# Late q tiles through DRAM, and re-timed loads and transposes around two attention turns

## The chip, the cores and the metric

The kernel runs on one core of a Trainium2 chip. The metric is the device time of one execution in microseconds (us), median of several runs. Five engines work side by side, each in the order of its own program: TensorE (PE, with weight loads shown as PEld), VectorE (DVE), ScalarE (ACT), GpSimd (POOL) and SyncE (SP). SP's queue (SPq) issues nearly all transfers (DMA), also those that transpose on the way. ACT's queue issues some.

## The reference, cut to what matters

One layer on 2048 tokens of width 640, forward and backward: linear attention with 32 heads of 20, then a gated MLP of width 1728, each behind a layer norm and with a residual. The outputs are the layer's result and the gradients for x, wqkv, wo, w1, w3 and w2.

```python
q, k, v = split_heads(layernorm(x) @ wqkv)
phi = lambda t: jnp.where(t > 0, t + 1, jnp.exp(t)) + 1e-6
pq, pk = phi(q), phi(k)
kv  = einsum("bhsd,bhse->bhde", pk, v)          # one 20x20 block per head
z   = einsum("bhsd->bhd", pk)
num = einsum("bhqd,bhde->bhqe", pq, kv)
den = einsum("bhqd,bhd->bhq", pq, z)[..., None] + 1e-6
h   = x + (num / den).reshape(S, D) @ wo
n   = layernorm(h)
out = h + (silu(n @ w1) * (n @ w3)) @ w2
# and the vjp of out for grad_out, in A_x, wqkv, wo, w1, w3, w2
```

The kernel never forms num. It makes r = pq / den for each tile of 128 tokens, and one matrix W' = blockdiag(kv) @ wo, so that the attention's result is r @ W'. In the backward pass Q' = r^T @ g_h takes the place of the sums over q: the gradient of kv, that of wo and the matrix for k's gradient come out of it.

## The kernel before

All is one program; the order of the Python calls is the order in each engine's queue. Tiles of a tag share buffers; `bufs` says how many. A new tile of a tag waits until the last reader of the buffer's previous tile is done. The forward turn begins when the last k tile is done: M = pk^T @ xn is formed in five blocks, transposed to mT by DMA, and kv follows from it.

```python
pqs[t] = p1.tile([P, D], BF16, name="pq", bufs=5)            # q tiles 0 to 4
...
def r_prod(t):                                              # POOL: pq * z
    for j in range(2):
        pr[t, j] = pf.tile([P, HD], F32, name="pr", tag="h2", bufs=3)
        G.tensor_tensor(out=pr[t, j][:], in0=pqs[t][:, js], in1=Zb[:, js], op=ALU.mult)

def r_rest(t):                                              # DVE: den, 1/den, r
    for j in range(2):
        V.reduce_sum(out=den[:, j * 16:(j + 1) * 16], in_=heads(pr.pop((t, j))[:]), axis=AX.X)
    V.tensor_scalar(out=den[:], in0=den[:], scalar1=1e-6, scalar2=None, op0=ALU.add)
    V.reciprocal(out=rden[:, t, :], in_=den[:])
    V.tensor_tensor(out=heads(pqs[t][:]), in0=heads(pqs[t][:]),
                    in1=rden[:, t, :].unsqueeze(2).to_broadcast([P, H, DH]), op=ALU.mult)

def r_out(t):                                               # SP: r^T for the product, r for later
    dmaT(out=pqT[:, :, t * P:(t + 1) * P], in_=pqs[t][:])
    dma(out=r_v[:, t, :], in_=pqs.pop(t)[:])

def q_late(t):                                              # q tiles 5 to 15
    pqs[t] = pf.tile([P, D], BF16, name="pql", bufs=4)
    for j in range(2):
        p1_half(acc[:, 0:HD], t, j * HD)                    # PE, 5 matmuls of 128x320
        A.activation(mq[:, js], acc[:, 0:HD], AF.Exp)
        A.activation(rq[:, js], acc[:, 0:HD], AF.Relu)
    V.tensor_scalar(out=mq[:], in0=mq[:], scalar1=1.0, scalar2=1e-6, op0=ALU.min, op1=ALU.add)
    V.tensor_tensor(out=pqs[t][:], in0=mq[:], in1=rq[:], op=ALU.add)

def f2_Wp():                                                # W' transposed, all five at the end
    for i in range(DT):
        dmaT(out=Wp[:, :, i * P:(i + 1) * P], in_=wTs[0][:, i, :])
    ...
# f2_at(t): x += r @ W' (PE, ACT or DVE), then statistics (DVE, POOL)
# f2_hn(t): layer norm (DVE), stored; f2_ht(t): its transposition (PE for t < 4, else DMA)
run((q_late, 5), (q_late, 6), (r_rest, 4), (q_late, 7), (r_out, 4), (r_prod, 5), (f2_kv, 3), (f2_kv, 4), (q_late, 8),
    (r_rest, 5))
Wp = U1.tile([P, DT, D], BF16, name="Wp", tag="W6")         # wo's buffer
run((f2_wT, 0), ..., (f2_wT, 4), (f2_Wp,), (r_out, 5), (r_prod, 6), (q_late, 9),
    (r_rest, 6), (r_out, 6), (r_prod, 7), (q_late, 10), (r_rest, 7), (r_out, 7), (r_prod, 8), (q_late, 11),
    (mlp_ghh, 4), (r_rest, 8), (f2_at0, 0), ..., (f2_hn, 0), (r_out, 9), ..., (f2_ht, 0), ...)
```

The MLP follows in four chunks of 512 tokens, 14 steps (`fc`) each. In chunk 0, `r_prod`, `r_rest` and `r_out` of tiles 12 to 15 stand between the steps; chunk c computes the attention of chunk c + 1.

In the backward pass, after the MLP's gradients, 16 tiles give g_h and g_q. Then Q' is summed (`q_parts`), and its transposition QT, wo, kvN (kv's) and W's parts are loaded or transposed for what follows:

```python
dmaT(out=woT, in_=A_wo[:, :])
load_xnT(0); load_wqT(2); load_xnT(1)
dmaT(out=kvN[:], in_=kvT_d[:, :])
... part(...)                                               # q_parts: each finished m issues dmaT(QT[m])
next(jobs)                                                  # a weight-gradient job: 16 matmuls of 128x320
for i in range(DT):
    dwoT.append(br.tile([P, D], BF16, name="dwoT", bufs=2))
    unload(square(qp, kvN, i), dwoT[i][:], (A.copy, V.tensor_copy)[i % 2])
    dmaT(out=dwo[:, :, i * P:(i + 1) * P], in_=dwoT[i][:])
A.dma_start(out=out3S, in_=dwo[:])
next(jobs)
for m, (a, b) in enumerate(M_H):                            # gkvT = wo^T-block @ QT
    acc = d_acc()[:, 0]                                     # tag dkv, three buffers, as in square()
    ...; masked(gkvT, acc[:, 0:n], m)
...
for i in range(DT):
    unload(square(wqT[:, 2 * DT:, :], gkvT, i), gm[:, i, :], ...)
    dmaT(out=wqT[:, 2 * DT:, i * P:(i + 1) * P], in_=gm[:, i, :])
for m in range(DT):
    dmaT(out=gkv_b[:, :, m * P:(m + 1) * P], in_=gkvT[:, m, :])
for t in range(ST):                                         # the g_k loop: xn @ gm, jobs between;
    ...                                                     # at t = 2, 5, 8, 11, 14: square(mN, gkv_b, n)
```

Of the kernel before, what the change touches and what calls it, by code (L numbers as in the profile page):

```python
# [50 lines left out]
SQ = _pieces(M_H, SPLIT_D, DH)  # L51


@with_exitstack
def kernel(
# [22 lines left out]
    def rows(ap):  # L78
        return ap.rearrange("(t p) d -> p t d", p=P)
# [9 lines left out]
    dram = ctx.enter_context(tc.tile_pool(name="dram", bufs=1, space=bass.MemoryType.DRAM))  # L89
    r_d = dram.tile([S, D], BF16, name="r_d")  # L90
# [4 lines left out]
    kvT_d = dram.tile([D, D], BF16, name="kvT_d")  # L95
    hn_d = dram.tile([S, D], BF16, name="hn_d")
    hh_d = dram.tile([F, S], BF16, name="hh_d")
    gg_d = dram.tile([2 * F, S], BF16, name="gg_d")
    r_v, pk_v, xn_v, hn_v, m_v = rows(r_d), rows(pk_d), rows(xn_d), rows(hn_d), rows(m_d)
# [117 lines left out]
    mT = p1.tile([P, DT, D], BF16, name="mT")  # L217
# [82 lines left out]
    def r_prod(t):  # L300

        for j in range(2):
            js = slice(j * HD, (j + 1) * HD)
            pr[t, j] = pf.tile([P, HD], F32, name="pr", tag="h2", bufs=3)
            G.tensor_tensor(out=pr[t, j][:], in0=pqs[t][:, js], in1=Zb[:, js], op=ALU.mult)
# [35 lines left out]
    mbs = pf.tile([P, 4, D], BF16, name="mbs", tag="hnT")  # L341
# [9 lines left out]
    def m_end(m):  # L351
        mb = mbs[:, m % 4, :]
        acc = macc.pop(m)
        for j in range(2):
            A.copy(out=mb[:, j * HD:(j + 1) * HD], in_=acc[j][:, 0:HD])
        dmaT(out=mT[:, :, m * P:(m + 1) * P], in_=mb)
        dma(out=m_v[:, m, :], in_=mb)
# [101 lines left out]
    m_part(2, range(8))  # L459
    z_sum(*zz)  # L460
    r_prod(0)
    m_part(2, range(8, ST))
    m_end(2)
    r_rest(0)
    r_prod(1)
    p1_kv(0)
    m_part(3, range(8))
    r_out(0)
    r_rest(1)
    r_prod(2)  # L470
    m_part(3, range(8, ST))
    m_end(3)
    p1_kv(1)
    r_out(1)
    r_rest(2)
    r_prod(3)
    m_part(4, range(8))
    p1_kv(2)
# [32 lines left out]
    def q_late(t):  # L511

        mq, rq = (p1.tile([P, D], BF16, name=n, bufs=b) for n, b in (("mq", 3), ("rq", 4)))
        pqs[t] = pf.tile([P, D], BF16, name="pql", bufs=4)
        for j in range(2):
            acc = ps.tile([P, 512], F32, name="mm", bufs=4)
            js = slice(j * HD, (j + 1) * HD)
            p1_half(acc[:, 0:HD], t, j * HD)
# [4 lines that stand above are left out]
# [3 lines left out]
    def f2_wT(i):  # L526

        if i == 0:
            wTs[0] = p1.tile([P, DT, D], BF16, name="wTs", tag="pk")
        acc = [ps.tile([P, 512], F32, name="wt", tag=("o2", "at")[i % 2], bufs=2) for _ in range(2)]  # L530
        for c, a, b, bank, off, first in SQ:
            T.matmul(acc[bank][:, off:off + (b - a) * DH], lhsT=wo[:, c, i * P:(i + 1) * P],
                     rhs=bd[:, c, a * DH:b * DH], start=first, stop=True, skip_group_check=True)
        for bank, (a, b), eng in ((0, (0, SPLIT_D), A.copy), (1, (SPLIT_D, H), V.tensor_copy)):
            eng(out=wTs[0][:, i, a * DH:b * DH], in_=acc[bank][:, 0:(b - a) * DH])

    def f2_Wp():
        for i in range(DT):
            dmaT(out=Wp[:, :, i * P:(i + 1) * P], in_=wTs[0][:, i, :])
        dma(out=rows(wT_d), in_=wTs[0][:])  # L540
        dma(out=rows(kvT_d), in_=bd[:])

# [5 lines left out]
    def f2_ht(t):  # L548
        c, i = divmod(t, TPC)
        if i == 0:  # L550

            hnT[c] = (pf.tile([P, DT, W], BF16, name="hnT", tag="hnT") if c == SC - 1 else pqT[:, :, c * W:(c + 1) * W])
        if t >= TPC:
            dmaT(out=hnT[c][:, :, i * P:(i + 1) * P], in_=hn[t][:])
            return
        tr = ps.tile([P, DT, P], BF16, name="trh", tag="mm", bufs=4)
        for d in range(DT):
            T.transpose(tr[:, d, :], hn[t][:, d * P:(d + 1) * P], ident[:])
        A.copy(out=hnT[c][:, :, i * P:(i + 1) * P], in_=tr[:])
# [76 lines left out]
    def o2_steps(c, q=dma, tag="o2"):  # L636
# [4 lines left out]
        for n, (i, j, fc) in enumerate(jobs):  # L641
            if fc == 0:
                o2["ps"] = ps.tile([P, 512], F32, name="o2", tag=tag, bufs=2)
                if j == 0:
                    o2["sb"] = pf.tile([P, D], BF16, name="h2", bufs=3)
# [25 lines left out]
    def run(*steps):  # L671
# [3 lines left out]
    run((q_late, 5), (q_late, 6), (r_rest, 4), (q_late, 7), (r_out, 4), (r_prod, 5), (f2_kv, 3), (f2_kv, 4), (q_late, 8),  # L675
        (r_rest, 5))
    Wp = U1.tile([P, DT, D], BF16, name="Wp", tag="W6")
    run((f2_wT, 0), (f2_wT, 1), (f2_wT, 2), (f2_wT, 3), (f2_wT, 4), (f2_Wp,), (r_out, 5), (r_prod, 6), (q_late, 9),
        (r_rest, 6), (r_out, 6), (r_prod, 7), (q_late, 10), (r_rest, 7), (r_out, 7), (r_prod, 8), (q_late, 11),
        (mlp_ghh, 4), (r_rest, 8), (f2_at0, 0), (r_out, 8), (r_prod, 9), (q_late, 12), (f2_at0, 1), (r_rest, 9), (f2_hn, 0),  # L680
        (r_out, 9), (r_prod, 10), (q_late, 13), (f2_ht, 0), (f2_at0, 2), (f2_x, 4), (r_rest, 10), (f2_hn, 1),
        (r_out, 10), (r_prod, 11), (q_late, 14), (f2_ht, 1), (f2_at0, 3), (f2_hn, 2), (w2T_rest, 8 * P), (mlp_ghh, 5),
        (r_rest, 11), (r_out, 11), (q_late, 15), (f2_ht, 2), (f2_hn, 3), (f2_x, 6), (mlp_ghh, 6), (load_g2T, 1), (f2_ht, 3),
        (mlp_ghh, 7))
# [20 lines left out]
    for c in range(SC):  # L705
# [8 lines left out]
        for fc in range(FT):  # L714
# [13 lines left out]
            if c == 0 and fc >= 2 and fc < 14:  # L728
                u, k = divmod(fc - 2, 3)
                (r_prod, r_rest, r_out)[k](12 + u)  # L730
# [11 lines left out]
            if c == SC - 1 and fc == 9:  # L742
                wT2 = U1.tile([P, DT, D], BF16, name="wT2", tag="W6")
                dma(out=wT2[:], in_=rows(wT_d))
# [100 lines left out]
    gkv_b = bd  # L845
# [25 lines left out]
    def ln_bwd(acc, t, nrm, st, out, res, pl):  # L871

        gs = pl.tile([P, D], BF16, name="gs", bufs=2)
# [11 lines left out]
        def rest():  # L885
            y = pl.tile([P, D], BF16, name="y")
            A.activation(out=y[:], in_=wb[:], func=AF.Identity, bias=s[:, 3:4], scale=st.rs[:, t:t + 1])  # L887
            V.tensor_tensor(out=out, in0=y[:], in1=res, op=ALU.add)
# [83 lines left out]

    b_load(0)
    b_load(1)
    for t in range(ST):
        g = b_ghn(t)

        def part():
            next(g, None)
# [21 lines left out]
        if t >= 4:  # L1001
            load_xn(t - 4, t - 3)


    tri = U1.tile([P, 3 * DT, D], BF16, name="tri", tag="S0")
    woT, QT, qp = (tri[:, k * DT:(k + 1) * DT, :] for k in range(3))
    kvN = br.tile([P, DT, D], BF16, name="kvN")
# [7 lines left out]
    part()  # L1015
    ln_rest.pop(a)()
# [6 lines left out]
    dmaT(out=woT, in_=A_wo[:, :])  # L1023
    load_xnT(0)
    load_wqT(2)
    load_xnT(1)
    dmaT(out=kvN[:], in_=kvT_d[:, :])
    b_gT(b)
# [8 lines left out]
    part(3)  # L1037
    load_xnT(2)
    load_xnT(3)
# [5 lines left out]
    obs = U1.tile([P, OB], BF16, name="obs", tag="W6")  # L1045
# [28 lines left out]
    jobs = wq_jobs((0,))  # L1074

# [16 lines left out]
    dwo = br.tile([P, DT, D], BF16, name="dwo")  # L1092
    dwoT = []
    for i in range(DT):
        dwoT.append(br.tile([P, D], BF16, name="dwoT", bufs=2))
        unload(square(qp, kvN, i), dwoT[i][:], (A.copy, V.tensor_copy)[i % 2])
        dmaT(out=dwo[:, :, i * P:(i + 1) * P], in_=dwoT[i][:])
    A.dma_start(out=out3S, in_=dwo[:])
    next(jobs)
# [12 lines left out]
    mN, gkvT, gm = (small[:, n:n + DT] for n in (0, DT, 2 * DT))  # L1112
    gzd = small[:, 3 * DT, :].rearrange("p (m q) -> p m q", q=P)
    G.memset(gkvT, 0.0)
    gzb = dx.tile([P, D], F32, name="gzb")
    for m, (a, b) in enumerate(M_H):
        n = (b - a) * DH
        acc = d_acc()[:, 0]
        for c in range(DT):
            T.matmul(acc[:, 0:n], lhsT=woT[:, c, m * P:(m + 1) * P], rhs=QT[:, c, a * DH:b * DH], start=(c == 0),  # L1120
                     stop=(c == DT - 1))
        masked(gkvT, acc[:, 0:n], m)
# [11 lines left out]
    for m in range(DT):  # L1134
        dmaT(out=gkv_b[:, :, m * P:(m + 1) * P], in_=gkvT[:, m, :])

# [4 lines left out]
    for x, y, bank in ((0, 4 * P, 0), (4 * P, D, 1)):  # L1141
        A.copy(out=gzb[:, x:y], in_=acc[:, bank, 0:y - x])
    next(jobs)

    for t in range(ST):
# [6 lines left out]
        gp = dx.tile([P, D], F32, name="gp", bufs=2)  # L1152
# [45 lines left out]
    def e_gxn(t):  # L1198
# [6 lines left out]
        gx = ex.tile([P, D], BF16, name="gx", bufs=2)  # L1205
        ln_bwd(acc, t, xnN[:, t, :], ln1, gx[:], g_h[:, t, :], ex)()
# [5 lines left out]
    jobs = wq_jobs((1,))  # L1212
    for t in range(3):
        for k in range(2):
            next(jobs)
            e_T(t, k)
    for t in range(ST):
# [6 lines left out]
        dma(out=out1S[:, t, :], in_=gx[:])  # L1224
# [10 lines left out]
    njob = 8  # L1235
    for i, (_, out, f0) in enumerate(blocks):
# [39 lines left out]
```

## Time and profile before

| what | value |
|---|---|
| device time, median of 3 | 920.9 us (920.63 to 924.73) |
| span of the profiled run | 922.1 us |
| TensorE busy | 838.3 us, 91% |
| VectorE busy | 454.1 us, 49% |
| ScalarE busy | 322.6 us, 35% |
| GpSimd busy | 101.0 us, 11% |
| q tiles, m, kv, W' and the first attention tiles | about 58 to 162 us |
| forward MLP | 162 to 413 us |
| backward MLP | 413 to 613 us |
| Q', dwo, gkvT, gm, g_k | 613 to 714 us |
| x's gradient and the last weight gradients | 714 to 922 us |

The page cuts the span into 40 slices and gives each engine's busy share in tenths, and in the line PEclk the clock that TensorE was granted. A timeline line has the start, the duration, the engine, the source line, the operation with output and inputs, the number of instructions, and in brackets the idle time before it with the work that ended it. A line of waits has who waited for whom, the microseconds in total, how often, and the longest. The chain of waits is followed back from the last instruction: at each step to what released it.

### The profile page before, as it was taken

How to read it: one execution, taken by the hardware profiler on the slowest of the kernel's cores; microseconds unless marked ns; L12 is line 12 of the kernel's file. 1: busy time of each engine (PE TensorE's matmuls, PEld its weight loads, DVE VectorE, ACT ScalarE, POOL GpSimd, SP SyncE). 2: the span in 40 equal slices, each digit the busy share in tenths (PEclk: the TensorE clock that was granted, in tenths of full speed). 3: DMA queues.
4: the chain of work that ended last, by engine and by line, in shares of the span. 5: the costliest groups of instructions: out<-in, count | busy, mean ns of one | idle time of the engine just before them, and what ended most of it. 6: DMA issues, size and time to landing. Idle time of an engine off the chain costs nothing.

```text
span 922.1 us, 13964 instructions
## 1 busy us (share of the span) xinstructions
PE 838.3 (91%) x5463; PEld 527.0 (57%) x5463; DVE 454.1 (49%) x921; ACT 322.6 (35%) x619; POOL 101.0 (11%) x119
## 2 busy tenths in 40 slices
PE   6987615999999999999999999998669999999998
PEld 4655403444555555577777777766437777655554
DVE  7967254689677675650015777771236245500000
ACT  4843303776555556611121121121202234311111
POOL 3673021220000000000001111111000000000000
PEclk9999857999999999999999999999779999999999
DMA  9996524586633444689976876539779479857581
GB/s 252 272 307 162 122 57 116 159 226 174 172 120 91 140 129 153 203 196 256 248 201 149 208 171 156 148 80 199 180 137 228 99 170 216 172 125 176 129 192 39
DMA packets 336243, 155.13 MB, mean 168 GB/s; under 512 B 239024, under 2 KB 334896, under 8 KB 336176
## 3 DMA queue, kind: packets, MB, share of 16 engines
q1 hardware_dynamic: 317824, 143.82, 64.2%
q10 hardware_dynamic: 18352, 10.41, 5.1%
q8 instruction: 43, 0.70, 0.3%
q14 instruction: 24, 0.20, 0.1%
HBM read 46.84 MB, written 49.33 MB: 104 GB/s over the span
## 4 chain that ended last, share of the span: by engine, by line
PE 73%; DVE 7%; SPq 5%; DMA 3%; issue 2%; ACT 2%; DVEq 0%; ACTq 0%
PE job L1053 17%; PE mm L327 15%; PE ghn L864 13%; PE gxn L1203 7%; PE o L646 6%; PE gw L816 6%; PE gr L920 2%; PE dkv L1150 2%; DMA r_d<-pql 2%; PE at L503 1%; SPq L971 1%; DVE den L313 1%; SPq L320 1%; DMA dwo<-dwoT 1%; DVE s L622 1%
## 5 line engine op out<-in xcount | busy, mean ns | idle before, releaser
L1053 PE MATMUL job<-gb,hnN 128*128 128x432 bf16 x640 | 117.0, 346 | 0.0
L864 PEld LDWEIGHTS <-ggb 128*128 128x128 bf16 x864 | 84.5, 98 | 32.8
L327 PE MATMUL mm<-pqT,w 128*128 128x512 bf16 x405 | 95.9, 383 | 1.8 <-ACT gate L588 0.9
L1053 PEld LDWEIGHTS <-hnN 128*128 128x128 bf16 x640 | 62.6, 98 | 54.1
L327 PEld LDWEIGHTS <-w 128*128 128x128 bf16 x540 | 53.2, 99 | 67.0 <-issue 5.8
L1057 ACT CAST obs<-job 128x432 bf16<-128x432 f32 (+1 forms) x60 | 29.2, 486 | 137.8 <-PE job L1053 134.7
L646 PE MATMUL o<-w,hhT 128*128 128x320 bf16 x448 | 67.5, 299 | 0.0
L327 PE MATMUL mm<-g2T,w2T 128*128 128x512 bf16 x260 | 65.7, 384 | 0.2 <-ACT gate L588 0.2
L864 PE MATMUL ghn<-w13a,ggb 128*128 128x320 bf16 x448 | 63.5, 299 | 0.0
L864 PE MATMUL ghn<-w13b,ggb 128*128 128x320 bf16 x416 | 61.4, 299 | 0.0
L646 PEld LDWEIGHTS <-hhT 128*128 128x128 bf16 x448 | 43.8, 98 | 23.6
L816 PE MATMUL gw<-g,hb 128*128 128x320 bf16 x416 | 57.0, 299 | 0.0
L887 ACT ACTIVATE y<-wb,s,ln_rs 128x640 bf16<-128x640 f32 x32 | 29.5, 921 | 66.5 <-DVE wb L883 66.5
L337 ACT CAST ghh<-mm 128x512 bf16<-128x512 f32 x52 | 30.6, 588 | 57.4 <-PE mm L327 48.9
L928 POOL TENSOR_TENSOR sz<-Zb,g_h 128x640 f32<-128x640 bf16 x16 | 20.2, 1262 | 271.3 <-DVE g_h L926 271.3
L816 PEld LDWEIGHTS <-hb 128*128 128x128 bf16 x416 | 40.6, 98 | 15.7
L1203 PE MATMUL gxn<-wqT,gT 128*128 128x320 bf16 x320 | 48.7, 299 | 0.0
L142 POOL TENSOR_TENSOR ln_rs<-ln_ve,mhalf 128x1 f32<-128x1 f32 x32 | 23.6, 736 | 202.3 <-DVE ln_ve L140 202.1
L242 PEld LDWEIGHTS <-pqT 128*128 128x128 bf16 x320 | 33.5, 107 | 17.6 <-DMA pqT<-x_sb 1.1
L586 ACT ACTIVATE sig<-mm 128x512 bf16<-128x512 f32 x56 | 33.6, 600 | 25.7 <-PE mm L327 23.4
L327 PEld LDWEIGHTS <-w2T 128*128 128x128 bf16 x280 | 27.5, 99 | 26.1 <-issue 1.3
L1053 PEld LDWEIGHTS <-g 128*128 128x128 bf16 x320 | 32.3, 101 | 14.0 <-issue 0.3
(160 smaller groups left out, 1254.1 us busy)
## 6 DMA issues: line engine op xcount, KB each, us to landing
hh_d<-hhT SPq DMA_DIRECT2D x24, 256.0 KB, 2.6
gg_d<-gate SPq DMA_DIRECT2D x24, 256.0 KB, 2.3
gg_d<-up SPq DMA_DIRECT2D x24, 256.0 KB, 2.2
ggb<-gg_d SPq DMA_DIRECT2D x6, 896.0 KB, 5.6
ggb<-gg_d SPq DMA_DIRECT2D x6, 832.0 KB, 5.9
out_dram<-obs ACTq DMA_DIRECT2D x40, 108.0 KB, 2.5
ggb<-gg_d SPq DMA_DIRECT2D x2, 1728.0 KB, 13.4
x_sb<-in_A_x_dram SPq DMA_DIRECT2D x5, 640.0 KB, 5.0
```

Source lines behind the costliest of these rows:

```text
L142: G.tensor_tensor(out=self.rs[:, a:b], in0=self.ve[:, a:b], in1=mhalf[:, 0:b - a], op=ALU.pow)
L242: T.matmul(acc, lhsT=pqT[:, c, t * P:(t + 1) * P], rhs=wqkv[:, c, n0:n0 + HD], start=(c == 0), stop=(c == DT - 1))
L327: T.matmul(acc[:], lhsT=w[:, c, fc * P:(fc + 1) * P], rhs=rhs[:, c, :], start=(c == 0), stop=(c == DT - 1))
L337: A.copy(out=ghh[n // 2][:, n % 2, :], in_=acc[:])
L586: A.activation(sig[:, i, :], gp[:], AF.Sigmoid)
L646: T.matmul(o2["ps"][:, 0:HD], lhsT=hhT[c][:, fc, i * P:(i + 1) * P], rhs=w2[:, fc, j * HD:(j + 1) * HD], start=(fc == 0), stop=(fc == FT - 1))
L816: T.matmul(acc[:, j, 0:HD], lhsT=hb[b][:, t, i * P:(i + 1) * P], rhs=g2[:, t, j * HD:(j + 1) * HD], start=(t == 0), stop=(t == ST - 1))
L864: T.matmul(acc[:, j, 0:HD], lhsT=ggb[t // 2][:, k, lo:lo + P], rhs=rhs[:, j * HD:(j + 1) * HD], start=(k == 0), stop=(k == NG - 1))
L887: A.activation(out=y[:], in_=wb[:], func=AF.Identity, bias=s[:, 3:4], scale=st.rs[:, t:t + 1])
L1053: T.matmul(acc[:, 0:n], lhsT=lhs[:, t, m * P:(m + 1) * P], rhs=rhs(t), start=(t == 0), stop=(t == ST - 1))
L1057: A.copy(out=ob, in_=acc[:, 0:n])
L1203: T.matmul(acc[:, j, 0:HD], lhsT=g, rhs=wqT[:, k, j * HD:(j + 1) * HD], start=(k == 0), stop=(k == 14))
```

## The change

It is made for the two stretches in which TensorE is not full. Forward: q tiles 8 to 15 are stored in DRAM as they are and read back in the first two MLP chunks, where r is made of them; the transposition of W' is issued block by block, W' no longer takes wo's buffer, and the last block of M is transposed on TensorE. Backward: wo and kvN are loaded earlier, gkvT is computed ahead of dwo, dwo is transposed through DRAM in the last stretch, and the blocks of `gkv_b` are transposed on TensorE.

```diff
+    pq_d = dram.tile([S, D], BF16, name="pq_d")
+    dwoT_d = dram.tile([D, D], BF16, name="dwoT_d")
-    mT = p1.tile([P, DT, D], BF16, name="mT")
+    mT = U1.tile([P, DT, D], BF16, name="mT", tag="MW")
-            pr[t, j] = pf.tile([P, HD], F32, name="pr", tag="h2", bufs=3)
+            pr[t, j] = pf.tile([P, HD], F32, name="pr", tag=tag, bufs=bufs)      # "h2", 2
+        if m < DT - 1:
+            dmaT(out=mT[:, :, m * P:(m + 1) * P], in_=mb)
 # q_late
-        pqs[t] = pf.tile([P, D], BF16, name="pql", bufs=4)
+        pqs[t] = (pf.tile([P, D], BF16, name="pql", bufs=4) if t >= 8 else p1.tile([P, D], BF16, name="pq", bufs=5))
 # f2_wT: both copies on ACT, and
+        dmaT(out=Wp[:, :, i * P:(i + 1) * P], in_=wTs[0][:, i, :])
+    def f2_mT():
+        for c in range(DT):
+            T.transpose(tr[:, c, :], mbs[:, 0, c * P:(c + 1) * P], ident[:])
+        A.copy(out=mT[:, :, (DT - 1) * P:], in_=tr[:])
+    def q_out(t):
+        dma(out=pq_v[:, t, :], in_=pqs.pop(t)[:])
+    def r_load(t):
+        pqs[t] = pf.tile([P, D], BF16, name="pql", bufs=4)
+        dma(out=pqs[t][:], in_=pq_v[:, t, :])
+    Wp = U1.tile([P, DT, D], BF16, name="Wp", tag="MW")
+    run((q_late, 5), (f2_mT,), (q_late, 6), (r_rest, 4), (r_prod, 5), (f2_kv, 2), (f2_kv, 3), (f2_kv, 4), (q_late, 7),
+        (f2_wT, 0), (f2_wT, 1), (r_out, 4), (q_late, 8), (r_rest, 5), (r_prod, 6), (f2_wT, 2), (f2_wT, 3), (q_late, 9),
+        (f2_wT, 4), (r_out, 5), (q_out, 8), (q_late, 10), (r_rest, 6), (r_prod, 7), (q_out, 9), (q_late, 11), (r_out, 6),
+        (q_out, 10), (q_late, 12), (r_rest, 7), (mlp_ghh, 4), (q_out, 11), (f2_at0, 0), (r_out, 7), (q_late, 13),
+        (f2_w_out,), (q_out, 12), (f2_at0, 1), (f2_hn, 0), (q_late, 14), (f2_ht, 0), (q_out, 13), (f2_at0, 2), (f2_x, 4),
+        (f2_hn, 1), (f2_ht, 1), (mlp_ghh, 5), (q_out, 14), (f2_at0, 3), (f2_hn, 2), (w2T_rest, 8 * P), (q_late, 15),
+        (f2_ht, 2), (f2_hn, 3), (f2_x, 6), (mlp_ghh, 6), (q_out, 15), (load_g2T, 1), (f2_ht, 3), (mlp_ghh, 7))
 # in the MLP steps
-            if c == 0 and fc >= 2 and fc < 14:
-                u, k = divmod(fc - 2, 3)
-                (r_prod, r_rest, r_out)[k](12 + u)
+            if c < 2:
+                u, k = divmod(fc, 3)
+                if k == 0 and u > 0:
+                    r_out(7 + 4 * c + u)
+                if u < 4:
+                    (r_load, lambda t: r_prod(t, "pql", 4), r_rest)[k](8 + 4 * c + u)
 # backward MLP loop over tiles
+        if t == 9:
+            dmaT(out=woT[:], in_=A_wo[:, :])
+        if t == 11:
+            dmaT(out=kvN[:], in_=kvT_d[:, :])
 # q_parts: xn 1, 2, 3 follow QT's blocks instead of standing before them; after it
+    gkvT = bd
     next(jobs)
+    next(jobs)
+    for m, (a, b) in enumerate(M_H): ...; masked(gkvT, acc[:, 0:n], m)           # moved ahead of dwo
+    dwoT = U1.tile([P, DT, D], BF16, name="dwoT", tag="W6")
     for i in range(DT):
-        unload(square(qp, kvN, i), dwoT[i][:], (A.copy, V.tensor_copy)[i % 2])
-        dmaT(out=dwo[:, :, i * P:(i + 1) * P], in_=dwoT[i][:])
+        unload(square(qp, kvN, i), dwoT[:, i, :], A.copy)
+    dma(out=rows(dwoT_d), in_=dwoT[:])
 # gkv_b
-        dmaT(out=gkv_b[:, :, m * P:(m + 1) * P], in_=gkvT[:, m, :])
+    for c, ms in SQ_BLOCKS:
+        for i, m in enumerate(ms):
+            T.transpose(tr[:, i, :], gkvT[:, m, c * P:(c + 1) * P], ident[:])
+        V.tensor_copy(out=gkv_b[:, c, ms[0] * P:(ms[-1] + 1) * P].rearrange("p (i q) -> p i q", q=P), in_=tr[:])
 # last stretch
+    dmaT(out=g_h[:, 0:DT, :], in_=dwoT_d[:, :])
+    dma(out=out3S, in_=g_h[:, 0:DT, :])
```

Cut from it: the order of M's blocks in the turn (block 2 is formed whole before the z sum, block 3 before kv 0), buffer counts (`h2` 3 to 2, `gp` 2 to 1), and `scr`, a tile of wo's old buffer in which the last layer norm's backward keeps its three intermediates.

## The prediction

> **What bounds the kernel now.** I read the slices of the page first, then busy time by stretch, then TensorE's waits, and last the queue that each long wait leads to.
>
> ```profile
> PE   6987615999999999999999999998669999999998
> ...
> PEclk9999857999999999999999999999779999999999
> ```
>
> A slice is 23.05 us. TensorE is full except at the start, in slices 2 to 6 (the forward attention turn) and in 27 to 29 (the backward one), and the granted clock falls in the same places. The three dense stretches (forward MLP, backward MLP, final weight gradients) hold nothing to win, and the change touches them only at their edges. Busy time by stretch (columns: length, then busy of PE, weight load, DVE, ACT, POOL, then granted clock, DMA share, GB/s):
>
> ```profile
> 81.00:108.00 27.00, 22.23 (x159) 15.01 (x157) 12.42 (x29) 14.39 (x38) 3.92 (x6) 0.87 0.66 166
> 108.00:136.00 28.00, 0.98 (x9) 0.50 (x7) 15.41 (x37) 3.50 (x10) 6.44 (x9) 0.60 0.27 48
> 136.00:162.00 26.00, 16.17 (x80) 9.07 (x80) 10.64 (x28) 8.43 (x18) 2.78 (x4) 0.70 0.50 124
> 219.00:284.00 65.00, 64.97 (x358) 34.98 (x358) 48.00 (x91) 38.23 (x72) 3.70 (x4) 1.00 0.52 146
> 642.00:661.00 19.00, 7.63 (x53) 5.52 (x51) 3.15 (x12) 2.08 (x6) 0.00 (x0) 0.64 0.64 120
> 661.00:684.00 23.00, 13.91 (x109) 9.55 (x107) 6.64 (x10) 4.62 (x13) 0.00 (x0) 0.84 0.93 200
> ```
>
> From 108 to 136 no engine is busy: DMA 0.27, DVE 15.4 of 28. That is a chain of latencies, not a full engine. TensorE's waits name its two ends:
>
> ```profile
> PE trh L558 <- DVE hn L145: 36.9, 3, 27.0
> PE dkv L1120 <- ACT dwoT L1089: 10.7, 2, 7.5
> PE dkv L1083 <- DMA bd<-small: 8.9, 4, 5.8
> ```
>
> The 36.9 us are followed into DVE's timeline:
>
> ```profile
> 111.60 0.49 DVE L522 TENSOR_TENSOR pql<-mq,rq 128x640 bf16<-128x640 bf16 x1 [12.64 <-DMA r_d<-pql]
> ...
> 118.24 0.49 DVE L522 TENSOR_TENSOR pql<-mq,rq 128x640 bf16<-128x640 bf16 x1 [3.21 <-DMA r_d<-pql]
> ```
>
> DVE runs in order. A late q tile takes one of four `pql` buffers and gives it back only when its r has been made (DVE), transposed and stored (SP queue, DMA). The steps are written so that tile t+4 asks for the buffer that tile t has hardly begun to give back: one turn round the ring costs 6.6 us a tile (111.60 to 118.24). The layer norm of the first MLP tiles stands behind this in DVE's queue, so TensorE's transposes of hn wait. DVE's list of waits has 33.5 us in 7 such waits.
>
> In the backward turn the chain of waits runs through the SP queue:
>
> ```profile
> 618.97 3.15 SPq L971
> ...
> 622.16 4.84 SPq L1021
> ...
> 640.62 1.22 SPq L955
> ...
> 646.52 2.62 DMA dwo<-dwoT
> ...
> 678.75 2.65 DMA bd<-small
> ```
>
> From 614 to 679 SP issues transposes almost without a break. The ones that TensorE needs (QT at L955, dwo, then `gkv_b`) stand behind wo, W', xn and kvN.
>
> **What the skill says.** "DMA: Bandwidth & Descriptors", section "Two DMAs through the same engine are not ordered": the ordering to be had is the completion semaphore. So a buffer is free, and the reload of q from DRAM may start, only once the store has landed. The trace agrees: the store r_d<-pql at 116.06 releases DVE at 118.24, 2.1 us later. "TensorE: Matmul & The Clock Gate", "What's actually happening": an idle stretch drops the clock to half. The trace agrees: ten matmuls of 128x320 take 2.19 us at 139.60, after the hole, and 1.52 at 149.19. "Perfetto Trace Analysis", "What \"DMA-bound\" means": one form is an issuing sequencer solid with DMA slices. SP is in that form at 614 to 679. "DMA: Bandwidth & Descriptors", "Silent corruption: two transposing streams in flight at once": transposes issued from SP and from ACT must not overlap, which matters for part 4.
>
> **The change, part by part.**
>
> 1. Late q. Tiles 8 to 15 no longer make r in the turn: each is stored as it is (one store of about 0.58 us of issue, 2.1 us to land) and its buffer is free. Tiles 5 to 7 use the pool of five. The r work of eight tiles leaves DVE's queue here, 8 x 2.7 us (86.02 to 88.72, the two sums to the product), and with it eight issues of 1.2 + 0.58 us on SP. The ring is gone.
>
> What is left sets the length. TensorE's work between 81.4 and 161.8 is, at full clock: 11 q tiles x 1.36, 4 chunks of ghh x 1.08, 4 attention tiles x 1.63, transposes 4 x 0.28, kv and W' 2.4: 15.0 + 4.3 + 6.5 + 1.1 + 2.4 = 29.3 us, in 80.3. Idle takes 42, the slow clock the rest.
>
> I laid the new steps out on the engines with the spacings of the trace (ACT 1.36 a q tile; DVE 0.83 a q tile, 2.7 an r, 1.23 a set of statistics, 0.36 a norm). M's product no longer stops for the z sum as long, and the fourth transposition is done on TensorE, so that the first late q tile starts at about 76 rather than 81.4. Then the waits that I find: W' needs all of kv masked by DVE, which is behind on r of tiles 1 to 4: 4 us. The first attention tile needs W' landed and ACT through with four q tiles: 1 us. The transposes of hn 0, 1 and 2 wait for attention copy, statistics and norm: 3 + 2 + 1 us. With 30 us of work (kv 2 and the mT transposes are added) that is 41 to 42, so the MLP would start at 118 rather than 161.8: 44 us. I take 2 off for a slow clock after the small waits: **42 us**.
>
> 2. r in the first two chunks. Chunk 0 had four r tiles already (12 to 15, now 8 to 11), so it only gains loads. Chunk 1 gains four: 11 us on a DVE that is busy 48.0 of 65.0 us, so 59 of 65. It fits by the sum, but DVE now waits in order for a load, a POOL product of 2 x 0.79 and then reduces. I put **2 us** of loss on it.
>
> 3. Backward turn. SP loses kvN and wo (3.4 + 4.6 us) and the five transposes each of dwo and of `gkv_b`. By SP's durations QT's last transposition is issued at 613.8 + 0.6 + 3.1 + 4.8, then, once the q sums are there, five of 1.25 and three xn of 2.9: about 639, landed at 640.5. TensorE ends its sums at 635.9 and has two jobs of 2.17 first, to 640.2. So gkvT starts at 640 rather than 650. The five squares for dwo are unloaded by ACT alone (5 x 0.75), a job and the gm squares follow, and the 13 small PE transposes with five DVE copies cost about 1 us. The g_k loop starts at 653.5 rather than 665.3: 12 us. In the loop the 9 us of wait for bd<-small are gone, and about 1 us of half clock in it: **21 us** with 1 us taken off for the copies' PSUM buffers.
>
> 4. wo and kvN in the backward MLP loop. SP has room there, and TensorE is full for 140.6 of 141 us. These are SP transposes between ACT's ghT ones, so each side waits for the other. A ghT may go out some 2.5 us late, and it has about 5 us to spare (landed 3.8 after its issue, read near 9). Cost 0, at most 2.
>
> 5. dwo's transposition goes to the last stretch, and SP is free there: 0. `h2` with two buffers, `gp` with one (both its users are on DVE), scr: 0.
>
> Sum: 921 - 42 + 2 - 21 = 860; with half of the 2 us of part 4, **861 us**.
>
> **The rivals.** (a) ACT, DVE and TensorE all have about 30 us of work in the shortened turn, so in-order queues may trade waits and the MLP starts at 128 to 133: about 873. For it speaks that kv's masks stand behind r on DVE; against it, that ACT and DVE each have under 32 us to do. (b) The r work in chunk 1 stalls DVE, and through the gate and up buffers TensorE, by 2 to 3 us a tile in eight tiles: up to 20 us back, 880. For it: DVE 59 of 65 us, and stores on SP that wait for DVE ahead of the q loads. Against: in chunk 0 four such tiles already ran with TensorE busy 55.05 of 57 us. (c) The SP queue stays the bound in the backward turn, as gm's five transposes, W' loads and pkT are crowded into less time: half of the 21 us lost, 871. Against: SP's chain loses 8 + 13 us of issue there. (d) It goes slower, because q stored through DRAM is waited for. That needs over 60 us of new waits; the stores are done a whole stage ahead of their loads.
>
> **Range and chances.** The holes are measured, and nothing fills them but the waits I listed. Taking (a) and half of (b) gives 883, the turn without my 4 + 6 us of waits and no loss in the chunks gives 848. Range **848 to 884**. Over 2% faster means under 902.5, that is more than 18 us; the forward hole of 27 us alone is more: 0.94. Within 2%: 0.04. Slower: 0.02.
>
> **What would show it.** No wait of DVE pql on r_d, and hn's wait under 8 us in all. The first MLP matmul near 118 to 122; chunk 1 still at about 65 us with DVE near 59. QT's last transposition issued at about 639; no wait on bd<-small; the g_k loop beginning some 12 us nearer to the end of the q sums. Wrong it would be if DVE's waits on r_d came back as POOL waits on pq_d, if SP were solid through 614 to 679 as before, or if the backward MLP loop grew.

## The result and the profile after

The changed kernel takes 863.7 us (median of 4 runs, 862.68 to 864.67), beside 921.25 us of the kernel before on the same chip (median of four executions, the three of the table above among them). The ratio is 0.9368, with a 95% interval of 0.9342 to 0.9394. The prediction was 861 us.

The slices of the page of the changed kernel, each 21.6 us:

```profile
PE   6998789899999999999999999899899999999998
...
PEclk9999899999999999999999999999999999999999
```

The two holes have closed to slices of 7 and 8, and the granted clock falls in one slice instead of five. TensorE's longest waits (who waited for whom, microseconds in total, how often, longest):

```profile
PE tr L239 <- DVE x_sb L148: 7.7, 3, 5.5
PE trh L572 <- DVE hn L148: 7.3, 2, 5.4
PE gr L935 <- DMA ghT<-g_h: 3.7, 2, 2.4
PE mm L330 <- ACT gate L602: 2.8, 4, 2.1
PE gkvT L1118 <- DMA tri<-tri: 1.9, 1, 1.9
PE wt L534 <- DVE bd L196: 1.8, 1, 1.8
```

The first line is the start of the kernel, which the change does not touch. The wait for hn went from 36.9 us to 7.3. Of the 10.9 us of waits for ACT's copies of dwoT 0.3 are left, and the 8.9 us for bd<-small are gone. The third line is new: in the kernel before, the matmuls of `gr` waited for nothing but 0.8 us of an ACT copy.

Where the time went is read from where each stage begins in TensorE's timeline. All numbers are microseconds; the last column is how much the stage that ends at this row has changed in length:

| stage begins | before | after | earlier by | change since the row above |
|---|---|---|---|---|
| forward MLP, chunk 0 | 161.8 | 117.5 | 44.3 | -44.3 |
| chunk 1 (its first matmul for the output) | 215.4 | 174.2 | 41.3 | +3.0 |
| gradient of w2 | 412.8 | 371.1 | 41.8 | -0.5 |
| backward MLP loop | 472.4 | 430.7 | 41.8 | 0.0 |
| Q' sums | 608.8 | 572.8 | 36.1 | +5.7 |
| first job after the sums | 635.9 | 598.9 | 37.0 | -1.0 |
| g_k loop | 665.3 | 617.6 | 47.7 | -10.6 |
| first job of g_k | 714.2 | 654.0 | 60.1 | -12.5 |
| last weight gradients | 801.4 | 742.1 | 59.3 | +0.9 |

So there are two gains, 44.3 us forward and 24.1 backward (1.0 + 10.6 + 12.5), and two losses: 3.0 us in the first MLP chunk and 5.7 in the backward MLP loop.

### The profile page after: what moved, and what is told of

It is laid out like the page before. It is cut to its first block, busy times and chain, and to the rows that moved or that the text cites. A ratio compares the mean times of both kernels' runs of the same rounds, so it can differ in the third digit from the quotient of the medians.

```text
span 862.3 us, 14041 instructions
## 1 busy us (share of the span) xinstructions
PE 826.8 (96%) x5481; PEld 521.7 (61%) x5481; DVE 449.8 (52%) x917; ACT 324.9 (38%) x629; POOL 98.3 (11%) x118
## 4 chain that ended last, share of the span: by engine, by line
PE 75%; DMA 5%; DVE 3%; SPq 2%; ACT 1%; issue 1%; POOL 0%; ACTq 0%; DVEq 0%; POOLq 0%
PE job L1073 18%; PE mm L330 15%; PE ghn L878 11%; PE gxn L1222 8%; PE o L660 7%; PE gw L831 7%; PE gwo L963 3%; PE gr L935 2%; PE dkv L1169 2%; PE at L505 2%; DMA ghT<-g_h 1%; DMA kvN<-kvT_d 1%; DMA woT<-in_A_wo_dram 1%; DMA pql<-pq_d 1%; DMA gg_d<-up 1%; SPq L209 1%
## 5 line engine op out<-in xcount | busy, mean ns | idle before, releaser
L878 PEld LDWEIGHTS <-ggb 128*128 128x128 bf16 x864 | 84.9, 98 | 33.5
L1222 PE MATMUL gxn<-wqT,gT 128*128 128x320 bf16 x320 | 48.9, 299 | 0.1
L890 ACT ACTIVATE gs<-ghn 128x640 bf16<-128x640 f32 x16 | 11.2, 703 | 83.7 <-PE ghn L878 67.7
L245 PEld LDWEIGHTS <-pqT 128*128 128x128 bf16 x320 | 31.7, 101 | 16.2 <-issue 3.1
L1222 PEld LDWEIGHTS <-gT 128*128 128x128 bf16 x320 | 31.2, 98 | 12.5 <-DMA gT<-g_k 0.4
```

The source lines that it names most:

```text
L245: T.matmul(acc, lhsT=pqT[:, c, t * P:(t + 1) * P], rhs=wqkv[:, c, n0:n0 + HD], start=(c == 0), stop=(c == DT - 1))
L878: T.matmul(acc[:, j, 0:HD], lhsT=ggb[t // 2][:, k, lo:lo + P], rhs=rhs[:, j * HD:(j + 1) * HD], start=(k == 0), stop=(k == NG - 1))
L1222: T.matmul(acc[:, j, 0:HD], lhsT=g, rhs=wqT[:, k, j * HD:(j + 1) * HD], start=(k == 0), stop=(k == 14))
```

## The experiments

Each kernel ran with the kernel before on the same chip, and a ratio is always to that. Stage times are from the profiles. Up to the first late q tile the instructions are the same in the changed kernel and in its variants e5 to e11, and yet that tile began anywhere from 72.9 to 77.1 us. So stages are compared by their length, and differences of under 4 us in the total are not leaned on. Two lengths vary as well. The first chunk takes 55.0 to 56.7 us in the five kernels with the forward steps of the changed kernel, and 52.7 to 53.7 us in the three with those of before. The backward MLP loop takes 139.9 to 142.3 us in the six kernels that load wo and kvN early from SP's queue, and 136.4 us in the four that load them after the loop. The losses of 3.0 and 5.7 us are read from one pair of profiles; over all of them they are 1.3 to 4.0 us and 3.5 to 5.9 us.

**Each half alone.** The forward half keeps the backward steps of before, only with kvN, job outputs, `gp` and `scr` in the buffers of the changed kernel; the backward half keeps the old order of the forward steps.

```diff
 # e1: the changed kernel without
-        if t == 9: dmaT(out=woT[:], in_=A_wo[:, :])
-        if t == 11: dmaT(out=kvN[:], in_=kvT_d[:, :])
 # gkvT ahead of dwo, dwo through DRAM, gkv_b on TensorE, QT between the xn loads (all as before)
 # e2: the changed kernel without q_out and r_load, with the run(...) lists of before
```

> The kernel before with only the forward half of the change (backward steps as before; kvN and the job outputs only lie in other buffers). My theory, that the two halves are worth what their own stretches show and simply add: the MLP starts near 117.5 us as in the changed kernel, the first chunk is 3 us longer, all else is as before, so 921 - 44 + 3 = 880 us (877 to 884). Rival, that part of the backward stretch's gain comes from the forward half's buffers, or the other way round: under 874, or over 888.

> The kernel before with only the backward half of the change (forward steps in their old order; some buffers lie as in the changed kernel to make room, and two instead of three buffers for the pq*z products). My theory: 24 us won between the q sums and the last weight gradients, 5 to 6 us lost in the backward MLP loop to the early loads of wo and kvN, so 921 - 24 + 6 = 903 us (900 to 906). Rival, that the loop's loss is not due to the early loads but to what the forward half left: 897.

Measured: the forward half 883.7 us, ratio 0.9593 (0.9566 to 0.9620); the backward half 902.0 us, ratio 0.9790 (0.9765 to 0.9815). The gains add: (1 - 0.9593) + (1 - 0.9790) = 0.0617, where the whole change has 0.0632. In the forward half alone the MLP starts at 118.2 us, and the backward MLP loop takes 136.4 us as in the kernel before. In the backward half alone the loop takes 142.0 us, as in the changed kernel. So the loop's loss belongs to the backward half. TensorE's waits of the backward half alone still have the old hole:

```profile
PE trh L561 <- DVE hn L148: 36.3, 3, 25.6
```

**Was it the ring, or the work?** The r work left the turn, and so did the ring's round trip. This kernel keeps all the work in the turn, and changes only the order of the steps, so that r lags one tile behind instead of three.

```diff
 # e3: the kernel before, from r_out 5 on
-        (r_out, 5), (r_prod, 6), (q_late, 9), (r_rest, 6), (r_out, 6), (r_prod, 7), (q_late, 10), ...
+        (r_out, 5), (r_prod, 6), (r_rest, 6), (r_out, 6), ..., (r_rest, 8), (r_out, 8), (q_late, 9), (r_prod, 9),
+        (q_late, 10), (r_rest, 9), (r_out, 9), (r_prod, 10), (mlp_ghh, 4), (q_late, 11), (r_rest, 10), ...
```

> The kernel before, all work in the forward turn kept and no DRAM trip, but r of each late q tile made and stored one tile behind instead of three, so that a buffer of the ring is asked for only three tiles after it was given up. My theory, that the hole of 27 us was the ring's round trip: no wait of the late q tiles on the store of r longer than 5 us, the turn is then bound by DVE's 3.5 us a tile, the MLP starts at 131 to 138 us instead of 161.8, and the time is 891 to 898 us. Rival, that the r work itself (DVE and the SP queue) fills the turn whatever the order: 915 us or more.

Measured: 897.7 us, ratio 0.9754 (0.9728 to 0.9780), and the MLP starts at 136.5 us. DVE's waits of this kernel:

```profile
DVE pql L522 <- DMA r_d<-pql: 8.3, 1, 8.3
```

In the kernel before that was 33.5 us in 7 waits. One is left, longer than the 5 us I allowed it; it is the first one, for r 5, whose store is issued behind W's five transposes. From the first late q tile to the MLP it takes 57.6 us, where the kernel before takes 80.3 and the changed kernel 43.9: the same work in another order, with no buffer added, brings 22.7 of the 36.4 us. So over half of the hole was the ring. In the reordered kernel TensorE still waits for the first norm:

```profile
123.02 0.71 PE L558 MATMUL trh<-ident,hn 128*128 128x128 bf16 x5 [16.97 <-DVE hn L145]
```

My reading of the rest is DVE's own work, 2.7 us of r a tile that still stands ahead of the norms. No run shows that part by itself, nor what W's transposition block by block adds to it.

**The first chunk.** POOL's waits of the changed kernel:

```profile
POOL pr L308 <- DMA pql<-pq_d: 45.9, 7, 12.1
POOL pr L308 <- DVE den L316: 15.2, 6, 5.2
```

and DVE's timeline at the end of the chunk, where tile 11 is made:

```profile
168.78 0.49 DVE L316 TENSOR_REDUCE den<-pr 128x16 f32<-128x320 f32 x1 [3.97 <-POOL pr L308]
169.53 0.48 DVE L316 TENSOR_REDUCE den<-pr 128x16 f32<-128x320 f32 x1 [0.26 <-POOL pr L308]
```

DVE stands still for 4 us: SP issued the reload of q 11 at 163.8 us, behind the transposition and the store of r 10, and it landed at 167.8. TensorE stops at the same time, but its wait does not end on DVE. ACT's timeline and TensorE's:

```profile
168.60 0.58 ACT L602 CAST gate<-mm 128x512 bf16<-128x512 f32 x1 [3.49 <-DMA gg_d<-gate]
```

```profile
169.24 1.99 PE L330 MATMUL mm<-g2T,w2T 128*128 128x512 bf16 x5 [2.13 <-ACT gate L602]
```

TensorE waits for ACT to copy its sums out, and ACT for a store of the MLP itself (gg_d<-gate), which holds the buffer that the copy writes. DVE had the data of that store ready at 161.4 us. SP issued it at 164.3, behind the three transfers of r 10 and q 11, and it landed at 168.5, after all of them. In the whole run ACT's copies of gate wait 5.6 us for such stores, in the kernel before 1.9 us. So r's transfers in SP's queue are a cause to be weighed beside r's work. One kernel leaves the work out, another spreads it:

```diff
 # e5: r_prod and r_rest left out for tiles 8 to 11
-                if u < 4:
+                if u < 4 and (c == 1 or k == 0):
 # e9: one tile in every four steps, over three chunks
-            if c < 2:
-                u, k = divmod(fc, 3)
-                ...
+            u, k = divmod(c * FT + fc - 4, 4)
+            if 0 <= u < 8:
+                (r_load, lambda t: r_prod(t, "pql", 4), r_rest, r_out)[k](8 + u)
```

> The changed kernel with the product and the sums of r left out for tiles 8 to 11 in the first MLP chunk (q is still loaded, transposed and stored, and 1/den of these tiles is set to one, so the outputs are not the reference's). My theory, that the first chunk's 3 us of loss come from the wait of the POOL product for the reload and DVE's wait for it: the chunk returns to about 54 us and the time to 861 us or just under. Rival, that they come from the extra transfers among the chunk's stores and weight loads: the chunk stays at 56 to 57 us and the time at 863 to 864.

> The changed kernel with r of the late tiles spread evenly: one tile in every four MLP steps from the fifth step of the first chunk on, so that two tiles of r fall in the first chunk, four in the second and two in the third. My theory, that r's work in the first chunk costs TensorE about 7 us for four tiles and nothing in the second: the first chunk goes from 56.7 to 53 us (52 to 54.5), the second and third stay, and the ratio to the kernel before goes from 0.937 to 0.933. Rival, that the cost lies in the number of late q reloads queued behind stores, wherever they stand: the second or third chunk grows by what the first wins, ratio 0.937.

Measured: with the work left out 857.9 us, ratio 0.9299 (0.9261 to 0.9337), and the chunk takes 49.7 us instead of 56.7. That is below the 54 us I expected, since this kernel also leaves out what the kernel before had there. TensorE's timeline shows no wait in that chunk, though q is still loaded, transposed and stored: the transfers alone do not stop it. Spread, 858.8 us, ratio 0.9335 (0.9318 to 0.9351), and the chunk takes 50.3 us, below the 52 to 54.5 us I expected. The other three chunks together take 198.3 us beside 196.9, but they take 198.4 us as well in three kernels with the forward steps of the changed kernel (e1, e7, e11), so this says nothing of the spreading. POOL waits 49.0 us for reloads in the spread kernel, more than the 45.9 of the changed kernel, so these waits by themselves are not the loss. So r's work, packed as it is, cost the first chunk about 7 us in this profile (5 to 7 over all of them), and the kernel before had 3 to 4 us of that with its own four tiles. In the second chunk the same work costs nothing:

```profile
118.00:174.00 56.00, 52.16 (x247) 24.30 (x246) 42.31 (x81) 38.01 (x76) 10.85 (x12) 0.97 0.83 214
174.00:239.00 65.00, 65.00 (x359) 34.95 (x358) 57.42 (x114) 38.38 (x73) 10.67 (x12) 1.00 0.63 177
```

These are busy times of the changed kernel by stretch (length, then PE, weight load, DVE, ACT, POOL, clock, DMA share, GB/s), the first chunk and then the second. In the second DVE is busier, 57.4 of 65 us, and TensorE is full; in the first DVE has 14 us to spare, and TensorE is not. So it is not DVE's share that decides. The DMA share is 0.83 in the first chunk and 0.63 in the second. That r's work, as it stands among the first chunk's steps, costs the time is shown. Whether it does so through DVE's lateness, through r's transfers ahead of the MLP's stores in SP's queue, or through the traffic that delays their landing, is not: no run moves one of them alone.

**The early loads of wo and kvN.** ACT's timeline and SP's in the changed kernel, around the load of wo:

```profile
502.51 1.22 ACTq L915 DMA_TRANSPOSE ghT<-g_h  x1
...
516.81 1.22 ACTq L915 DMA_TRANSPOSE ghT<-g_h  x1
518.08 0.70 ACT L890 ACTIVATE gs<-ghn 128x640 bf16<-128x640 f32 x1 [7.86 <-issue]
```

```profile
510.58 4.01 SPq L1021 DMA_TRANSPOSE woT<-in_A_wo_dram  x1
```

The ghT transposes are 8.7 us apart elsewhere, so this one was due at 511.2. It went out at 516.8, when wo's had landed (6.1 us after its issue). It came 5.6 us late, and TensorE ran out of it twice, once for wo and once for kvN:

```profile
521.21 1.53 PE L935 MATMUL gr<-wT,ghT 128*128 128x320 bf16 x10 [1.26 <-DMA ghT<-g_h]
...
541.20 2.46 PE L935 MATMUL gr<-wT,ghT 128*128 128x320 bf16 x10 [2.43 <-DMA ghT<-g_h]
```

After the second gap the ten matmuls take 2.46 us instead of 1.53, and the next eighteen 3.40 instead of 2.61: the clock has dropped. Two kernels move the loads:

```diff
 # e6: both on ACT's queue, right behind b_gT
-        if t == 9: dmaT(out=woT[:], in_=A_wo[:, :])
+            if t == 9: A.dma_start_transpose(out=woT[:], in_=A_wo[:, :])
 # e11: both where they were before the change
+    dmaT(out=woT[:], in_=A_wo[:, :])
     load_xnT(0)
     load_wqT(2)
+    dmaT(out=kvN[:], in_=kvT_d[:, :])
```

> The changed kernel with the two early transposing loads (wo, kvN) issued from ACT's queue, right behind ACT's own transposition of g_h, instead of from SP's. My theory, that the backward MLP loop grew from 136.4 to 142.1 us because transposes of two queues wait for one another: with one queue the loop returns to 136.4 to 137 us and the time is 858 us (856 to 860). Rival, that the load itself (its traffic, or its 4 us of issue in front of ACT's next copy) holds the loop up: the loop stays at 140 us or more and the time at 862 or more.

> The changed kernel with wo and kvN loaded where they were before the change, after the backward MLP loop and ahead of QT in the SP queue. My theory, that the change paid 5.7 us in the loop for 7 to 8 us of SP time in the turn: the loop returns to 136.4 us, the last block of QT is issued 7 us later after the loop, the matmuls that wait for it too, and the time is 865 us (862 to 868), a ratio of 0.937 to 0.942. Rival, that the SP queue is no longer the bound in the turn: the time falls to 858.

Measured: on ACT's queue 860.1 us, ratio 0.9327 (0.9292 to 0.9363), and the loop takes 136.6 us. The total is 0.1 us above my range. The issue, 3.7 us here, now stands in front of ACT's next copy, and TensorE waits for none of it:

```profile
510.75 1.22 ACTq L915 DMA_TRANSPOSE ghT<-g_h  x1
512.01 3.72 ACTq L1011 DMA_TRANSPOSE woT<-in_A_wo_dram  x1
515.77 0.70 ACT L890 ACTIVATE gs<-ghn 128x640 bf16<-128x640 f32 x1 [6.01 <-issue]
```

This kernel moves the loads to another queue and to another moment, right behind a ghT. A load from SP's queue at that moment was not tried, so which of the two counts is open.

In the old place 868.3 us, ratio 0.9442 (0.9419 to 0.9465), just above the ranges I gave (862 to 868 us, 0.937 to 0.942). The loop takes 136.4 us again, and from the first job to the g_k loop it takes 25.6 us instead of 18.7. TensorE's timeline of that kernel shows why:

```profile
605.94 0.82 PE L1116 MATMUL gkvT<-tri,woT 128*128 128x160 bf16 x5 [5.06 <-DMA tri<-tri]
609.18 1.35 PE L1116 MATMUL gkvT<-tri,woT 128*128 128x140 bf16 x10 [2.42 <-DMA tri<-tri]
```

QT's last block is issued at 606.5 us, 10.7 us after the sums' end, instead of 2.8. So the early load paid for itself: 6.9 us won in the turn for 5.7 lost in the loop, 1.2 us by these two profiles and 1.0 to 3.4 us over the loop's spread. The ratios, 0.9368 and 0.9442, make it some 7 us, but between the two profiles 2.0 us lie in the forward turn, where the programs are the same. That it paid is shown, how much is not.

**gkv_b.** The kernel of the change with the old DMA transposes of gkv_b behind gm's:

```diff
 # e7
+    for m in range(DT):
+        dmaT(out=gkv_b[:, :, m * P:(m + 1) * P], in_=gkvT[:, m, :])
-    for c, ms in SQ_BLOCKS: ...                             # transposes on TensorE, copies on DVE
```

> The changed kernel with the blocks of gkv_b transposed by five DMA transposes behind gm's, as before the change, instead of on TensorE. My theory, that they stand in the SP queue behind gm's five: they land near 634 us, where the first square that reads them would run at 622.6 us, so 9 to 11 us are lost: 873 to 875 us. Rival, that the shortened SP queue hides them now: under 867 us.

Measured: 876.2 us, ratio 0.9496 (0.9467 to 0.9526). The g_k loop takes 48.9 us, exactly as in the kernel before, instead of 36.4. SP's and TensorE's timelines of this kernel:

```profile
615.62 10.98 SPq L1150 DMA_TRANSPOSE wqT<-small  x5
626.65 6.55 SPq L1152 DMA_TRANSPOSE small<-bd  x5
```

```profile
630.64 0.30 PE L1104 MATMUL dkv<-small 128*128 128x140 bf16 x1 [7.23 <-DMA small<-bd]
```

So all of the loop's 12.5 us come from these five transposes, which cost TensorE 1.2 us as matmuls. Without those the stage ahead of the loop is 1.7 us shorter (17.0 beside 18.7), so the balance is 10.7 us, within the 9 to 11 I expected; the total is 1.2 us above my range.

**The wait that is left forward.** DVE's timeline of the changed kernel:

```profile
97.46 0.49 DVE L524 TENSOR_TENSOR pql<-mq,rq 128x640 bf16<-128x640 bf16 x1 [2.98 <-DMA pq_d<-pql]
```

This is q 12 that waits for q 8's store: a remnant of the ring, as that store stands in SP's queue behind W's last three transposes and r 5.

```diff
 # e8
-        (f2_wT, 4), (r_out, 5), (q_out, 8), (q_late, 10), (r_rest, 6), (r_prod, 7), (q_out, 9), ...
+        (q_out, 8), (q_late, 9), (f2_wT, 4), (q_out, 9), (r_out, 5), (q_late, 10), (r_rest, 6), (r_prod, 7), ...
-        (q_late, 12), (r_rest, 7), ..., (f2_at0, 0), (r_out, 7), ...
+        (q_late, 12), ..., (f2_at0, 0), ..., (f2_hn, 1), (r_rest, 7), (f2_ht, 1), (r_out, 7), ...
```

> The changed kernel with q 8 and q 9 stored ahead of r 5 instead of behind it, and r of tile 7 made after the second layer norm instead of before the first. My theory, that the 5.4 us for which TensorE still waits for the first norm are DVE's 3.0 us of wait for the store of q 8 and the 2.7 us of r 7 that stand ahead of it: the wait falls under 1.5 us, the half-clock matmuls behind it go too, the MLP starts at 111 to 113 us instead of 117.5, and the time is 858 us (856 to 860). Rival, that ACT or POOL sets the first norm's time: no gain, 863 us.

Measured: 859.6 us, ratio 0.9315 (0.9283 to 0.9347). The MLP starts at 112.8 us, and 38.5 us after the first late q tile instead of 43.9. TensorE's transposes of hn wait 1.8 us for DVE in all, for the second norm, and not for the first.

**All three together** (e6, e8 and e9):

> The changed kernel with all three: the late r spread over three chunks, q 8 and q 9 stored earlier and r 7 later, wo and kvN loaded from ACT's queue. My theory, that the three act in three separate stretches and add: 4.7 us in the turn, 3 to 4 in the first chunk, 5.5 in the backward MLP loop, so 850 us (848 to 854) or a ratio of 0.923. Rival, that an earlier MLP start runs into the first chunk's weight loads: 855 or more.

Measured: 845.4 us, ratio 0.9188 (0.9168 to 0.9208), which beats both kernels and lies below the 848 to 854 us I expected. Beside the profile of the changed kernel the three stretches won 5.5, 6.6 and 5.7 us, about 18 in all; the first chunk won some 3 us more than I gave it. The slices:

```profile
PE   6988899999999999999999999998999999999998
...
PEclk9999999999999999999999999999999999999999
```

## Why the prediction was right

**Part 1, the forward turn: 42 us predicted, 44.3 measured.** The ring was the larger cause, as the removed waits and the reordered kernel show, and the length of the new turn followed from the work and the waits that the layout on the engines found. Of the 44.3 us, 36.4 are the turn itself. The other 7.9 lie ahead of its first late q tile, which came at 81.4 us before and at 73.6 after; it came at 78.9 to 81.4 us in the three kernels with the old steps there and at 72.9 to 77.1 with the new ones, so this part is 1.8 to 8.5 us, and no run tries it alone. Single terms were off and cancelled: the wait for kv's masks was 1.8 us, where I put 4; the first late q tile came at 73.6 us, where I put 76; the waits for hn were 7.8 us with ACT's, where I put 6. The layout missed that q 12 waits 3.0 us for q 8's store, since I looked at when the store could be issued and not at what stands ahead of it in SP's queue.

**Part 2, r in the chunks: 2 us predicted, 2.5 measured, but not where I put it.** I gave the loss to chunk 1, because DVE would be at 59 of 65 us there. DVE came to 57.4, and chunk 1 lost nothing. The 3.0 us were lost in chunk 0, where I counted no new work, only loads. TensorE's longest wait there ended on a store of the MLP that stood behind r's transfers in SP's queue. That the sum came out right is luck.

**Part 3, the backward turn: 21 us predicted, 24.1 measured.** gkvT began 4.3 us after the sums, as worked out. From the first job to the g_k loop it took 18.7 us, where I had 17.6. Of the 10.6 us won there, 6.9 come from wo and kvN leaving SP's queue (the kernel with both in the old place); the other 3.7, for gkvT ahead of dwo and dwo through DRAM, were not tried alone. The loop won 12.5 us, where I had 10. The waits for the five landings were 8.9 us, as I had them; the term that was undersized is the slow clock behind them, for which I took 1 us. In the kernel before:

```profile
681.63 2.87 PE L1150 MATMUL dkv<-small,xnT 128*128 128x320 bf16 x10
684.30 3.71 PE L1053 MATMUL job<-g_q,g 128*128 128x320 bf16 x16
687.84 2.88 PE L1150 MATMUL dkv<-small,xnT 128*128 128x320 bf16 x20
```

These 26 matmuls take 6.2 us from 681.63 to 687.84, and 3.5 us at the pace of the twenty that follow. The example of the slow clock in the prediction, 2.19 us beside 1.52, is not yet half. Right behind the hole five attention matmuls take 1.33 us to the start of the next (136.67 to 138.00), where 0.68 us is usual (102.87 to 103.55).

**Part 4, the early loads: 0 to 2 us predicted, 5.7 measured.** The mechanism was named and its size was wrong. I had ghT 2.5 us late with 5 us to spare; it was 5.6 us late. A load that lands 6.1 us after its issue makes ghT 2.5 us late only if it starts 3.6 us before that is due. But SP first issues the other loads of the same iteration, which wait for DVE (the last at 510.05), so that wo's began just before the next ghT was due (510.6 and 511.2). Then nearly all of its 6.1 us to landing is delay.

**The rivals.** (a), waits traded among the queues until 128 us, did not come: 117.5. (b), r stalling DVE in the chunks, is true in part: DVE did stall, and r's work held 3 us in the first chunk, 7 if the cost that the kernel before already had is counted, but TensorE's longest wait there did not end on DVE. (c), SP as the bound in the backward turn, did not come, and would have in part with wo and kvN in their old place: 7 us there. (d) did not come.

**The signs.** The good ones came: no wait of DVE pql on r_d, 7.3 us of wait for hn, the second chunk at 65 us with DVE at 57.4, no wait on bd<-small, and the last block of QT issued 2.8 us after the sums. The g_k loop began 10.6 us nearer to them, not 12. Of the three signs of being wrong, two came as well. POOL waited 45.9 us on pq_d; that was a poor sign, as the faster kernel with r spread has 49.0 us of it. And the backward MLP loop grew by 5.7 us; that was a true one, and is part 4. SP was not solid in the turn: from 605.0 to 610.8 us it issued nothing.

The sum, by the spans of the two profiles: 922.1 - 44.3 + 2.5 + 5.7 - 24.1 + 0.9 for the stretch of x's gradient - 0.5 for the last weight gradients, both of which I had at 0, is 862.3. The errors of parts 1 and 3 (5 us too careful) and of part 4 (5 us too easy) cancelled, so that the number came so close is luck; the mechanism of the two large parts is not.

## What to carry to other kernels

When no engine is full in a hole, look for a ring of buffers whose release lies several in-order queues away, and ask how many steps lie between the request and the release: the same work with the release brought forward gave over half of what the turn won, before anything was moved to DRAM. A store that is to free a buffer belongs in its queue ahead of transposes that nobody waits for yet. A transposing load put into a quiet stage is not free when another queue transposes there: what helped here, in the one loop where it was tried, was to put it on that queue, behind the transposition that is due.

## What the runs showed that I had not expected

The second chunk took 9.4 us more DVE work (57.4 us beside 48.0) with TensorE at 65.00 of 65 us, while the first chunk lost 7 us to the same work at a lower DVE share. And the start of the program, the same instructions in eight kernels, differed by 4 us from run to run (72.9 to 77.1 us to the first late q tile), which is more than several of the effects studied here. Later stages with no change in them differ in how well they repeat: the gradient of w2 took 59.6 us in all twelve kernels, the first job to the g_k loop's end 54.7 to 55.4 us in the seven with the same steps there, but the backward MLP loop 139.9 to 142.3 us in six. A single pair of profiles gives a stage's change no better than that.
